# Reordering VectorE's queue in both mixers of a fused attention and MLP block, and deferring one late ScalarE evacuation

## The chip, the cores and the metric

The kernel runs on one core of a Trainium2 chip. The metric is the device time of one execution in microseconds (us), the median of several runs. One execution was also profiled; the profile's span runs from the first to the last instruction and is about 1.8 us shorter than the metric. All runs told of here were with a granted TensorE clock of 0.999 to 1.0.

## The reference

The block is a linear attention layer followed by a token-mixing MLP, each behind a layer norm and with a residual. The change touches only the MLP:

```python
h = _layernorm(x)                                    # x: (1, 2048, 1024)
u = gelu(jnp.einsum("bsd,sf->bdf", h, w1) + b1)      # "mixer 1", 2048 -> 3584
y = jnp.einsum("bdf,fs->bds", u, w2) + b2            # "mixer 2", 3584 -> 2048
out = residual + y.transpose(0, 2, 1)
```

## The kernel before

Both mixers use a seven-product scheme in place of eight: each output block of 256x1024 is made from seven matrix products, some of which take sums or differences of operand blocks. VectorE makes those operand sums. Two output blocks form a "quad". Products 1, 5 and 3 of a quad are split once more into seven inner products of half width, for both blocks together; these are in1, in5 and in3 (mixer 1 also has in2). "Product 3 of in5" is the third-numbered inner product of outer product 5. Quads are numbered from 0, as in the code; quad 0 of mixer 2 uses no inner products, so quads 1, 2 and 3 are the three that the text speaks of there. Between the inner products, steps of an ordinary product of 512 columns fill TensorE.

The names in the profile: `sa` is an operand sum of an outer product (`asum(6)` in the code makes the one of product 6), `is` of an inner one, `wq` and `w2o` are weights, `gs` and `gi` (mixer 2) and `hi` (mixer 1) are sums on the moving side, `psI` holds the inner products in PSUM, `psA`, `psB`, `psC` the outer ones, `e`, `t` and `t1a` are partial sums in SBUF, `ot` is an output tile. Where its sum lies in `psA` or `psC`, it is made by an evacuation on ScalarE (a copy out of PSUM with the bias added) and then an addition of the residual `hr` on VectorE.

The inner products, in the order in which they are issued (cut):

```python
class Inner:
    def i1(self):   # ... a and b are the two halves that products 1, 2 and 6, 3 accumulate in
        ae = psz.tile([P, BANK], F32, tag="z0", ...); bc = psz.tile([P, BANK], F32, tag="z1", ...)
        # mixer 2 (banks == 2): a and e share one PSUM bank, b and c share another
        self.a, self.e, self.b, self.c = ae[:, 0:HW], e[:, HW:CW], bc[:, 0:HW], bc[:, HW:CW]
        self.mm(1, self.a, True)
        act.copy(self.b, self.a)
    # ... i6, i2, i5 ...
    def i7(self):
        self.mm(7, self.c, False)
        self.sink_sum(1, 1, self.c, self.es[:])      # VectorE addition that reads c
    def i3(self):
        self.mm(3, self.b, False)                    # TensorE writes b, in c's bank
        self.sink_sum(0, 1, self.b, self.es[:])
```

The interleaving. At each named point, deferred work ("late") is flushed if the point is listed, and then the action for that point is issued; numbers are stretches of filling steps:

```python
for f in (n.i1, "b", 0, n.i6, "c", n.i2, "2", 1, n.i5, n.i7, "7", 2, n.i3, "third", 3, n.i4, "end"):
```

One quad of mixer 2 (cut). VectorE's instructions keep the order in which they are written here:

```python
def run2(self, pend, on_p4, on_p7, cut, third_sums):
    def starting():
        self.asums(5)                  # sa, for both blocks
        self.in5 = self.inner(5)
        self.in5.sums()                # four is
        self.asums(6)                  # sa, for both blocks
        # ...
    self.interleave(self.in1, self.steps(*[st.p4 for st in pend]),
                    {"b": starting}, (("b", None), ("7", None), ("end", None)))
    on_p4()                            # two gs differences and their corrections
    # ...
    self.asums(7)                      # two wq differences, in place
    self.interleave(self.in5, self.steps(*[st.p6 for st in sts]))
    # ... asums(3), in3's sums, product 7 ...
    halves[0]()                        # a gs difference
    self.interleave(in3, self.steps(*[st.p2 for st in sts]),
                    {"2": halves[1], "7": begin_next, "third": before_last, ...}, (("7", None),))
```

The whole kernel:

## Time and profile before

| | before |
|---|---|
| time, median of the 3 runs not profiled | 567.18 us (566.92 to 568.14) |
| profiled span | 566.1 us |
| TensorE busy | 556.7 us, 98% |
| VectorE busy | 448.5 us, 79% |
| ScalarE busy | 287.6 us, 51% |
| gaps in TensorE's stream from 232 us on (why from there: last section) | 5.26 us |

The first part of the page gives engine, busy us, share of the span and instructions:

```profile
span 566.1 us, 8738 instructions
PE 556.7 (98%) x3278; PEld 309.8 (55%) x3278; DVE 448.5 (79%) x853; ACT 287.6 (51%) x609; POOL 1.8 (0%) x8
```

A TensorE that is busy 98% of the time looks as if 9 us were left, but pipelined matmuls overlap in the records (one of 512 columns is recorded as 379 ns long, and the next starts 216 ns after it), so the share says little about what is left. The Trainium skill says the same ("Perfetto Trace Analysis", section "Identifying the Most-Contended Engine": matmul busy share is not a good measure of how near TensorE is to its limit), and proposes other measures. Its section "Optimization Strategy" says to find the gaps between slices on the engine and what blocks it there. That is what we do. In the timeline, a group of n matmuls that starts at s should be followed by the next at s + n x pitch. The pitch is 0.216 us for 512 columns and 0.109 us for 256 (14 matmuls of 512 columns take 3.02 us, 14 of 256 take 1.53 us in the chain of waits). Whatever the next start lies beyond that is a gap.

The timeline of TensorE in mixer 2 (start, duration, engine, line, operation, output and inputs, count; in brackets the idle time before and what ended it):

```profile
439.97 1.24 PE L229 MATMUL psC<-gs,wq 128*128 128x512 f16 x5
442.11 0.92 PE L229 MATMUL psI<-gE,is 128*128 128x256 f16 x7 [0.90 <-DVE psA L229]
...
466.82 1.67 PE L229 MATMUL psA<-gO,w2o 128*128 128x512 f16 x7
469.42 0.92 PE L229 MATMUL psI<-gO,is 128*128 128x256 f16 x7 [0.93 <-DVE e L229]
...
470.94 1.24 PE L229 MATMUL psA<-gO,w2o 128*128 128x512 f16 x5
472.51 0.93 PE L229 MATMUL psI<-gO,is 128*128 128x256 f16 x7 [0.32 <-DVE e L229]
...
482.82 1.24 PE L229 MATMUL psC<-gs,w2o 128*128 128x512 f16 x5
484.17 0.92 PE L229 MATMUL psI<-gE,is 128*128 128x256 f16 x7
...
494.48 1.24 PE L229 MATMUL psB<-gT,sa 128*128 128x512 f16 x5
495.56 0.93 PE L229 MATMUL psI<-gE,is 128*128 128x256 f16 x7
```

The first pair reads: 439.97 + 5 x 0.216 = 441.05, the next group starts at 442.11, so the gap is 1.06 us. In the same way the others are 1.09, 0.49 and 0.27 us (and once more 0.27 us in quad 3, at 524.66). The last pair has no gap: 494.48 + 1.08 = 495.56. The gap of 0.27 us at 484.17 has no bracket, because the modelled ends of the matmuls before it cover it: counts and pitches find it, idle time does not.

In quad 1 of mixer 1 the same reading gives 0.52 us at 257.52 and 0.78 us at 279.21, and another 0.19 us at 275.16:

```profile
255.92 1.24 PE L229 MATMUL psC<-hT,wq 128*128 128x512 f16 x5
257.52 0.60 PE L229 MATMUL psI<-hi,is 128*128 128x256 f16 x4 [0.35 <-ACT psI L229]
...
278.00 0.59 PE L229 MATMUL psC<-hT,sa 128*128 128x512 f16 x2
279.21 0.60 PE L229 MATMUL psI<-hi,sa 128*128 128x256 f16 x4 [0.61 <-DVE t L229]
```

These gaps add up to 4.67 us: 0.52 + 0.19 + 0.78 in mixer 1, and 1.06 + 1.09 + 0.49 + 0.27 + 0.27 in mixer 2. The rest of the 5.26 us are seven gaps of 0.08 to 0.09 us.

At 257.52 TensorE waits for a copy of `psI` on ScalarE that stands behind a gelu, which itself waited for VectorE:

```profile
256.47 0.72 ACT L229 ACTIVATE gE<-e,b_sb 128x512 f16<-128x512 f32 x1 [0.61 <-DVE e L229]
257.10 0.36 ACT L229 COPY psI<-psI 128x256 f32<-128x256 f32 x1
```

The timeline of VectorE shows what stands in front of the additions that TensorE waits for, and where VectorE itself stands idle:

```profile
439.63 2.08 DVE L229 TENSOR_TENSOR sa<-sa,wq 128x1792 f16<-128x1792 f16 x2
441.64 0.42 DVE L229 TENSOR_TENSOR psA<-psI,es 128x256 f32<-128x256 f32 x1
...
445.31 0.42 DVE L229 TENSOR_TENSOR ot<-ot,hr 128x512 bf16<-128x512 bf16 x1 [1.80 <-ACT ot L480]
445.65 2.02 DVE L229 TENSOR_TENSOR gs<-gT,gE 128x3584 f16<-128x3584 f16 x1
...
467.02 2.01 DVE L229 TENSOR_TENSOR gs<-gO,gT 128x3584 f16<-128x3584 f16 x1
468.95 0.41 DVE L229 TENSOR_TENSOR e<-psI,e 128x256 f32<-128x256 f32 x1
...
476.96 0.42 DVE L229 TENSOR_TENSOR ot<-ot,hr 128x512 bf16<-128x512 bf16 x1 [0.45 <-ACT ot L480]
...
494.90 0.41 DVE L229 TENSOR_TENSOR e<-psI,es 128x256 f32<-128x256 f32 x1
```

The addition at 441.64 ends at 442.06, and product 3 starts at 442.11. It stood behind two `sa` sums that nobody needed yet. Product 3 writes the other half of the bank that this addition reads, and TensorE stands idle for 0.90 us before it. The Trainium skill ("PSUM — Partial Sum Buffer", section "PSUM bank collisions raise a hardware error") says to guard PSUM by bank (strictly, by bank and quadrant of partitions) and not by address; the wait in this trace fits that. In in3 the `e` addition at 468.95 ends at 469.36, behind a `gs` difference of 2 us, and the matmuls at 469.42 wait for it.

### The profile page before, as it was taken

To read this page: it belongs to the slowest core of one execution; us is meant where nothing else is said; L and a number is where in the kernel's file an instruction comes from. 1 tells how busy PE (TensorE), PEld (TensorE's weight loads), DVE (VectorE), ACT (ScalarE), POOL (GpSimd) and SP (SyncE) were. 2 spreads that over 40 slices of the span, in tenths; PEclk is the share of its full clock that TensorE was granted. 3 is DMA by queue.
4 is the path that set the end of the run, shared out by engine and by line. 5 is a ranking of instruction groups with operands and counts; after the bars stand their busy time and mean duration, and the time that the engine had idled before them with its cause. 6 is when DMAs were issued, how large, how long until landed. Compare 5 with 4: busy or idle time off the path is not lost.

```text
span 566.1 us, 8738 instructions
## 1 busy us (share of the span) xinstructions
PE 556.7 (98%) x3278; PEld 309.8 (55%) x3278; DVE 448.5 (79%) x853; ACT 287.6 (51%) x609; POOL 1.8 (0%) x8
## 2 busy tenths in 40 slices
PE   8999999999999999999999999999999999999997
PEld 3444444454444444456666766666445655656654
DVE  6898888544776788888989789888997889879783
ACT  4747777766766877635546465555211312313212
POOL 1000000000000000000000000000000000000000
PEclk9999999999999999999999999999999999999999
DMA  9833342115764862104041340431946644643111
GB/s 303 292 75 75 77 91 38 19 53 191 213 213 122 252 187 77 72 1 129 23 148 30 120 150 1 149 81 51 251 127 180 168 115 127 168 132 111 37 38 56
DMA packets 86217, 67.15 MB, mean 119 GB/s; under 512 B 15890, under 2 KB 80160, under 8 KB 86176
## 3 DMA queue, kind: packets, MB, share of 16 engines
q1 hardware_dynamic: 85440, 65.94, 39.9%
q10 hardware_dynamic: 672, 0.66, 0.3%
q8 instruction: 25, 0.41, 0.3%
q14 instruction: 16, 0.13, 0.1%
q0 software_dynamic: 64, 0.01, 0.0%
HBM read 54.54 MB, written 8.91 MB: 112 GB/s over the span
## 4 chain that ended last, share of the span: by engine, by line
PE 84%; DVE 10%; DMA 3%; issue 1%; ACT 1%; SPq 0%; DVEq 0%; ACTq 0%
PE psI L229 19%; PE acc_t L229 18%; PE psC L229 11%; PE psB L229 8%; PE psB L904 4%; PE psC L904 4%; PE psA L904 4%; PE psA L229 4%; DVE sa L229 2%; PE acc_t L1179 2%; PE psE L904 2%; DVE is L229 2%; PE psC L341 2%; PE psA L341 2%; PE acc_t L828 2%; DMA wkv<-in_A_wqkv_dram 1%
## 5 line engine op out<-in xcount | busy, mean ns | idle before, releaser
L229 PEld LDWEIGHTS <-is 128*128 128x128 f16 x652 | 63.6, 98 | 33.2 <-issue 5.6
L229 PEld LDWEIGHTS <-sa 128*128 128x128 f16 x606 | 59.3, 98 | 28.8 <-issue 0.9
L229 PEld LDWEIGHTS <-wq 128*128 128x128 bf16 (+1 forms) x503 | 49.2, 98 | 32.6
L229 PE MATMUL acc_t<-wo_sb,pqT 128*128 128x512 f16 x256 | 55.6, 379 | 0.0
L229 PE MATMUL acc_t<-xnT,wq_sb 128*128 128x512 bf16 x192 | 43.4, 379 | 0.0
L229 PEld LDWEIGHTS <-pqT 128*128 128x128 bf16 x256 | 25.0, 98 | 30.5 <-issue 0.6
L191 DVE TENSOR_SCALAR e_sb<-e_sb 128x512 bf16<-128x512 bf16 x64 | 18.5, 290 | 28.8 <-ACT e_sb L187 28.2
L187 ACT ACTIVATE e_sb<-acc_t 128x512 bf16<-128x512 f32 x40 | 23.9, 597 | 24.6 <-PE acc_t L229 12.0
L904 PEld LDWEIGHTS <-xs 128*128 128x128 f16 x208 | 20.0, 98 | 23.4 <-DVE xs L890 1.3
L229 PE MATMUL psC<-gs,wq 128*128 128x512 f16 x140 | 32.0, 379 | 0.0
L229 PE MATMUL psC<-hT,sa 128*128 128x512 f16 x112 | 31.2, 379 | 0.0
L229 PEld LDWEIGHTS <-wq_sb 128*128 128x128 bf16 x192 | 18.5, 98 | 23.0 <-issue 1.3
L229 PE MATMUL psI<-hi,is 128*128 128x256 f16 x200 | 30.0, 272 | 0.4 <-ACT psI L229 0.4
L229 PE MATMUL psB<-hT,sa 128*128 128x512 f16 x112 | 29.7, 379 | 0.0
L229 DVE BATCH_NORM_STATS2 hst<-acc_t 128x6 f32<-128x512 f32 x32 | 21.4, 692 | 9.1 <-ACT h_bf L229 8.9
L904 PE MATMUL psA<-wkv,xnT 128*128 128x512 bf16 x104 | 26.7, 379 | 0.0
L904 PEld LDWEIGHTS <-xnT 128*128 128x128 bf16 x156 | 15.3, 98 | 18.5 <-issue 0.2
L229 PE MATMUL psC<-hT,wq 128*128 128x512 f16 x96 | 24.6, 379 | 0.0
L229 ACT CAST h_bf<-acc_t 128x512 bf16<-128x512 f32 x32 | 18.4, 582 | 11.9 <-PE acc_t L229 11.2
L229 ACT COPY psI<-psI 128x256 f32<-128x256 f32 x50 | 17.9, 359 | 11.7 <-PE psI L229 10.6
L188 ACT ACTIVATE r_sb<-acc_t 128x512 bf16<-128x512 f32 x40 | 23.7, 593 | 0.0
L828 PE MATMUL acc_t<-wkv,xnT 128*128 128x512 bf16 x96 | 21.6, 379 | 0.9 <-ACT xnT L1081 0.9
(224 smaller groups left out, 1075.1 us busy)
## 6 DMA issues: line engine op xcount, KB each, us to landing
wq<-in_B_w_dram SPq DMA_DIRECT2D x14, 1024.0 KB, 7.8
wq<-in_B_w_dram SPq DMA_DIRECT2D x12, 896.0 KB, 6.4
xr<-in_A_x_dram SPq DMA_DIRECT2D x16, 256.0 KB, 5.8
rdb<-rd_dram SPq DMA_DIRECT2D x32, 128.0 KB, 3.9
h_dram<-h_bf SPq DMA_DIRECT2D x16, 256.0 KB, 2.0
hr<-h_dram SPq DMA_DIRECT2D x32, 128.0 KB, 3.2
out_dram<-ot SPq DMA_DIRECT2D x31, 128.0 KB, 2.1
x_sb<-in_A_x_dram SPq DMA_DIRECT2D x15, 256.0 KB, 3.1
```

Of the source, the lines that this page charges most:

```text
L187: pin(nc.scalar.activation(e_sb[:], src, ACT.Exp))
L188: pin(nc.scalar.activation(r_sb[:], src, ACT.Relu))
L191: pin(nc.vector.tensor_scalar(e_sb[:], e_sb[:], 1.0, PHI_EPS, ALU.min, ALU.add))
L229: return (lambda *a, **kw: pin(op(*a, **kw))) if self.always or getattr(Held, self.key) else op
L341: pe.matmul(ps[:, cols], lhsT=lhs[:, k, :], rhs=mv(k)[:, cols], start=(start and k == 0), stop=(k == self.nk - 1), skip_group_check=True,)
L828: mm = nc.tensor.matmul(pp[:, 0:CW], lhsT=xnT[:, kt, i * P:(i + 1) * P], rhs=wkv[:, kt, c * CW:(c + 1) * CW], start=(kt == 0), stop=(kt == ...
L904: pin(nc.tensor.matmul(ps[:], lhsT=lhs[:, k, :], rhs=rhs[:, k, :], start=(start and k == 0), stop=(k == hk2 - 1), skip_group_check=True,))
L1179: nc.tensor.matmul(qp[:, 0:SW], lhsT=wq_sb[:, kt, j * P:(j + 1) * P], rhs=xnT[:, kt, u * SW:(u + 1) * SW], start=(kt == 0), stop=(kt == ND ...
```

## The change

The intent is to keep operand sums that are needed late out of the way of additions that TensorE waits for. Sums of four are issued in halves, some of them behind those additions; the `gs` differences of in3 move one point later; of the two `sa` of `asum(6)` the second moves to the end of in1; and the gelu of mixer 1's first quad, second block, goes behind the next copy of `psI`. At point "b" of in1 only one deferred action is now flushed (`self.early`, 1, and 0 in quad 1, where none is waiting), so in quads 2 and 3 one `ot` addition, the one at 476.96 above, also goes behind the `psA` addition. No arithmetic is added. TensorE's order is unchanged; ScalarE's changes in that one place. The diff (cut to its core):

```diff
@@ run2
             def starting():
+                self.in1.sums(slice(2, 4))
                 self.asums(5)
                 self.in5 = self.inner(5)
-                self.in5.sums()
-                self.asums(6)
+                self.in5.sums(slice(0, 2))
+                sts[0].asum(6)
                 ...
             self.interleave(
-                self.in1, self.steps(*[st.p4 for st in pend]), {"b": starting}, (("b", None), ("7", None), ("end", None))
+                self.in1, self.steps(*[st.p4 for st in pend]),
+                {"b": starting, "7": lambda: self.in5.sums(slice(2, 4))}, (("b", self.early), ("7", None), ("end", None)),
             )
+            sts[1].asum(6)
             on_p4()
             ...
-            def before_last():
-                if nxt is not None:
-                    nxt.in1.sums(slice(2, 4))
-                sts[0].evac(0, 1, sts[0].e)
-
             def begin_next():
                 if nxt is not None:
                     nxt.in1 = nxt.inner(1)
                     nxt.in1.sums(slice(0, 2))
-
-            halves[0]()
+                sts[0].evac(0, 1, sts[0].e)
+
             self.interleave(in3, self.steps(*[st.p2 for st in sts]), {
-                "2": halves[1], "7": begin_next, "third": before_last,
+                "2": halves[0], "7": halves[1], "third": begin_next,
@@ run_first (mixer 1, first quad)
-            for st in sts:
-                st.p3()
+            sts[0].p3()
+            sts[1].p3_mm()
+            self.late.append(sts[1].p3_evac)
@@ run1 (mixer 1, second quad only: third_sums are the four sums on hO, "hi")
-                third_sums(slice(0, 2))
+                third_sums(slice(0, 3))
             ...
-            if third_sums is not None:
-                third_sums(slice(2, 3))
             ...
-                "b": nop if third_sums is None else lambda: third_sums(slice(3, 4)),
+                "7": nop if third_sums is None else lambda: third_sums(slice(3, 4)),
```

More of the change, by code (lines that the diff above doesn't have):

```diff
@@ L503, in __init__ @@
             self.S = {}
+            self.early = 1
         def cols(self, h):
@@ L1619 @@
     nxt = next2(1)
+    nxt.early = 0
     run_all(make_t4)
@@ L1622 @@
     nxt.in1 = nxt.inner(1)
-    nxt.in1.sums()
+    nxt.in1.sums(slice(0, 2))
     for st in pend:
```

## The prediction

> What bounds it. TensorE: the page's first part gives it 556.7 of 566.1 us (98%), VectorE 79%. Busy share can't say what is left, so I read the PE timeline. Matmuls start 0.109 us apart (256 columns) or 0.216 us (512); a gap is what a group's start lies beyond the start before plus count times pitch. Where the change acts I find:
> - mixer 1, quad 1: 0.52 us at 257.5 (copy of psI queued on ScalarE behind the late gelu), 0.19 at 275.2, 0.78 at 279.2 (VectorE "t" additions behind two "hi" sums);
> - mixer 2, quad 1: 1.06 at 442.1 (inner product 3 of in1, waits for the psA addition), 1.09 at 469.4 and 0.49 at 472.5 (in3, "e" additions behind a 2 us "gs" difference);
> - mixer 2, quads 2 and 3: 0.27 each at 484.2 and 524.7 (psA addition behind "sa" and "is").
> Together 4.67 us: the change cannot win more. The waits are for whole banks: product 3 writes one half of a PSUM bank whose other half the addition reads. That fits the Trainium skill, "PSUM — Partial Sum Buffer", section on bank collisions (guard by bank, not address); the trace shows 0.90 us of such idle at 442.1.
>
> What the change does. No arithmetic is added, PE's order stays; VectorE's instructions are permuted. Start to start in the VectorE timeline: is pair 1.1-1.2 us, sa 1.0, gs 1.95, inner addition 0.34, hi 0.6-0.7.
>
> Ledger:
> 1. Late gelu deferred: psI copy goes at about 256.1; 0.52 closes.
> 2. sums3: two hi leave the way of the t additions; 0.19 closes. But the fourth hi now stands after product 7's addition and product 4 needs it, about 0.5 us too late; of 0.78 only 0.25 is won. Items 1 and 2: about 0.95.
> 3. in1 of mixer 2: one sa and one is pair leave from before the psA addition: 1.06, 0.27, 0.27 close.
> 4. in3: gs goes behind the additions: 1.09 and 0.49 close; product 4 now needs the third addition, done just in time (margin under 0.05).
> 5. New cost. The second sa of asum(6) now comes after the ot addition that waits for ScalarE's last product-4 evacuation (idle 1.80 before it, each quad). That idle is not filled; instead gs, its corrections, two wq differences and the psI+es addition of in5 start 1.0 us later against PE. Before, from PE's last product-4 matmul to that addition's end takes 8.9 us, and product 3 of in5 follows after 9.1 (486.4 to 495.6): slack 0.2. So a gap of about 0.8 opens there in each of 3 quads: -2.45.
>
> Sum: 0.95 + 1.60 + 1.58 - 2.45 = about 1.7 us won: quad 1 gains about 1.8, quads 2 and 3 lose about 0.55 each.
>
> Predicted time: 565.5 us, range 563.3 to 567.0 (8 in 10). Faster by over 2%: 0.5%; within 2%: 99%; slower: 0.5%.
>
> What would show it. The gaps at 257.5, 442.1, 469.4, 472.5, 484.2, 524.7 gone from the PE timeline; about 0.5 us left near 278 with hi as cause; new waits of about 0.8 us on VectorE "e" at product 3 of in5 in all three quads of mixer 2; the mixer-2 quad period growing from 40.5 to about 41. VectorE busy unchanged.
>
> What would make it wrong. If the in5 addition has more slack than I read (ScalarE's evacuation earlier, so that idle is filled), the win is up to 4 us (563). If product 4 in in3 misses its margin, or output transfers hold a buffer, 0.3 to 1 us is lost per quad and the time is unchanged or slightly worse (567). The spread of runs before (566.92 to 568.14) is nearly the effect.

## The result

| | before | after |
|---|---|---|
| time, median of 4 runs each | 567.53 us (566.92 to 568.14) | 565.93 us (565.45 to 566.11) |
| profiled span | 566.1 us | 564.1 us |
| TensorE gaps from 232 us on | 5.26 us | 3.56 us |
| VectorE busy | 448.5 us | 448.3 us |

The ratio is 0.997 with a 95% interval of 0.9953 to 0.9988: 1.6 us faster, which is clear of noise. A ratio in this document is the mean time of one kernel's fast runs over that of the other's in the same rounds, so it is not quite the ratio of the medians. The gaps fell by 1.70 us. Of the 2.0 us that the profiled span shrank, the other 0.3 us lie before the first changed instruction: a gap of 0.08 us that both kernels have stands at 243.57 us before and at 243.27 us after. That much the unchanged first part moves from run to run.

The time alone is less sharp than its median looks: the interval of the ratio allows a gain of 0.7 to 2.7 us. The kernel before was run 27 more times beside the experiments below, with a median of 567.2 us, 1.3 us above the changed kernel's 565.9, and its profiled run (567.89) was one of its slow ones. The gaps are the better evidence.

The first part of the page, after:

```profile
PE 555.1 (98%) x3262; PEld 310.0 (55%) x3278; DVE 448.3 (79%) x853; ACT 287.4 (51%) x609; POOL 1.8 (0%) x8
```

The busy shares are those of before. TensorE's timeline of mixer 2 at the five places shown above:

```profile
438.73 1.24 PE L229 MATMUL psC<-gs,wq 128*128 128x512 f16 x5
439.81 0.93 PE L229 MATMUL psI<-gE,is 128*128 128x256 f16 x7
...
465.32 1.67 PE L229 MATMUL psA<-gO,w2o 128*128 128x512 f16 x7
466.84 0.93 PE L229 MATMUL psI<-gO,is 128*128 128x256 f16 x7
...
468.37 1.24 PE L229 MATMUL psA<-gO,w2o 128*128 128x512 f16 x5
469.44 0.93 PE L229 MATMUL psI<-gO,is 128*128 128x256 f16 x7
...
479.76 1.24 PE L229 MATMUL psC<-gs,w2o 128*128 128x512 f16 x5
480.84 0.93 PE L229 MATMUL psI<-gE,is 128*128 128x256 f16 x7
...
491.15 1.24 PE L229 MATMUL psB<-gT,sa 128*128 128x512 f16 x5
493.04 0.92 PE L229 MATMUL psI<-gE,is 128*128 128x256 f16 x7 [0.65 <-DVE e L229]
```

The four gaps of before are gone: 438.73 + 1.08 = 439.81, and so on. In their place there is a new gap where there was none: 491.15 + 1.08 = 492.23, and product 3 of in5 starts at 493.04, 0.81 us late. It stands in each of the three quads (452.01, 493.04 and 534.07), 2.43 us together. The time from one to the next, which is the length of a quad, is 41.03 us; before, it was 524.66 - 484.17 = 40.49 us.

VectorE's timeline in that quad shows why:

```profile
480.03 0.43 DVE L229 TENSOR_TENSOR psA<-psI,es 128x256 f32<-128x256 f32 x1 [0.78 <-PE psI L229]
...
484.03 0.42 DVE L229 TENSOR_TENSOR ot<-ot,hr 128x512 bf16<-128x512 bf16 x1 [1.50 <-ACT ot L480]
484.38 1.08 DVE L229 TENSOR_TENSOR sa<-sa,wq 128x1792 f16<-128x1792 f16 x1
485.38 2.02 DVE L229 TENSOR_TENSOR gs<-gT,gE 128x3584 f16<-128x3584 f16 x1
...
492.57 0.42 DVE L229 TENSOR_TENSOR e<-psI,es 128x256 f32<-128x256 f32 x1
```

The addition at 480.03 now waits for TensorE and not for operand sums. But `ot` waits 1.50 us for ScalarE's evacuation, and `sa`, which needs nothing from ScalarE, stands behind it. So `gs` starts 1.0 us later than directly behind `ot`, and with it the whole run up to the addition at 492.57. That addition ends at 492.99, and product 3 starts at 493.04.

In mixer 1 the gap at 257.5 is gone (255.62 + 1.08 = 256.70). The gap of 0.78 us has become one of 0.56 us, with another releaser:

```profile
255.62 1.24 PE L229 MATMUL psC<-hT,wq 128*128 128x512 f16 x5
256.70 0.60 PE L229 MATMUL psI<-hi,is 128*128 128x256 f16 x4
...
276.98 0.59 PE L229 MATMUL psC<-hT,sa 128*128 128x512 f16 x2
277.97 0.60 PE L229 MATMUL psI<-hi,sa 128*128 128x256 f16 x4 [0.39 <-DVE hi L229]
```

### The profile page after: what moved, and what is told of

The parts are those of the page before. It is cut to its first block, busy times and chain, and to the rows that moved or that the text cites. A ratio compares the mean times of both kernels' runs of the same rounds, so it can differ in the third digit from the quotient of the medians.

```text
span 564.1 us, 8722 instructions
## 1 busy us (share of the span) xinstructions
PE 555.1 (98%) x3262; PEld 310.0 (55%) x3278; DVE 448.3 (79%) x853; ACT 287.4 (51%) x609; POOL 1.8 (0%) x8
## 4 chain that ended last, share of the span: by engine, by line
PE 91%; DVE 6%; ACT 1%; issue 1%; DVEq 0%
PE psI L229 20%; PE acc_t L229 18%; PE psC L229 15%; PE psB L229 6%; PE psA L229 4%; PE psC L902 4%; PE psB L902 4%; PE psA L902 4%; DVE gs L229 3%; PE acc_t L826 3%; PE psB L341 2%; PE psA L341 2%; PE acc_t L1177 2%; PE psE L902 2%; PE psC L341 2%; PE kvps L855 1%
```

## The experiments

The theory: the new in5 gap comes from the second `sa` of `asum(6)` standing behind an `ot` addition that waits. Rival A: it comes from the other moved pair, the second half of in5's `is` sums, or from ScalarE's evacuation or transfers as such. Rival B: the split of `asum(6)` is what cured in1, so the gap is its price. All kernels below gave correct results. "Before" ran beside them, with medians of 567.1 to 567.2 us.

**e1: undo the split of asum(6).** Diff against the changed kernel:

```diff
-                sts[0].asum(6)
+                self.asums(6)
...
-            sts[1].asum(6)
             on_p4()
```

> Undo one part of the change: both sa operand sums of asum(6) again ahead of the psA addition; all else as after. My theory (the second sa behind an ot addition that waits for ScalarE makes the new gap): the 0.81 us gap at product 3 of in5 vanishes in all three quads, and because the is pair is now out of the way the psA addition still ends in time (computed 480.64 against 480.84 in the trace after), so no gap comes back at product 3 of in1, or under 0.05 us. Sum: 2.4 us under after, about 563.5 us. Rival A (the other part of the reordering, the second is pair of in5 moved behind the psA addition, or ScalarE/DMA, makes that gap): the in5 gaps stay at 0.8 and the time stays near 565.9. Rival B (the split of asum(6) is what cured in1): the 0.27 gaps at in1 come back, 0.5 to 1.5 us lost again.

Measured: 563.39 us (5 runs), ratio to before 0.9932 (0.992 to 0.9945). No in5 gap is left, and none came back at in1. Rivals A and B fall: with the rest of the change in place the split was not needed to cure in1, and it made the new gap.

**e2: swap two instructions.** The second `sa` is issued at the point "third", so that it stands directly ahead of the waiting `ot` and not behind it. Nothing else in any engine's order differs from the changed kernel.

```diff
-                {"b": starting, "7": lambda: self.in5.sums(slice(2, 4))}, (("b", self.early), ...
+                {"b": starting, "7": lambda: self.in5.sums(slice(2, 4)), "third": lambda: sts[1].asum(6)},
+                (("b", self.early), ...
             )
-            sts[1].asum(6)
```

> The only change in any engine's order against after: the second sa of asum(6) stands ahead of the ot addition that waits for ScalarE instead of behind it (six rows swap in the VectorE order). My theory: sa fills 1.0 of the 1.5 us idle there, gs starts 1.0 us earlier against PE, the three 0.81 us gaps at product 3 of in5 vanish: 2.4 us under after, about 563.5 us; VectorE busy unchanged. Rival A (is pair, or ScalarE or transfers): gaps stay, about 565.9 us.

Measured: 563.86 us (5 runs), ratio 0.9941 (0.9928 to 0.9953). VectorE busy is 448.3 us, as after. The VectorE timeline of the same quad:

```profile
482.02 1.08 DVE L229 TENSOR_TENSOR sa<-sa,wq 128x1792 f16<-128x1792 f16 x1
483.61 0.43 DVE L229 TENSOR_TENSOR ot<-ot,hr 128x512 bf16<-128x512 bf16 x1 [0.51 <-ACT ot L480]
483.95 2.02 DVE L229 TENSOR_TENSOR gs<-gT,gE 128x3584 f16<-128x3584 f16 x1
...
491.15 0.42 DVE L229 TENSOR_TENSOR e<-psI,es 128x256 f32<-128x256 f32 x1
```

And TensorE's:

```profile
490.73 1.24 PE L229 MATMUL psB<-gT,sa 128*128 128x512 f16 x5
491.81 0.93 PE L229 MATMUL psI<-gE,is 128*128 128x256 f16 x7
```

The idle time before `ot` shrank from 1.50 to 0.51 us, because `sa` ran in it. The addition ends at 491.57, before product 3 is due at 490.73 + 1.08 = 491.81. All three gaps are gone, for the same work. e1 and e2 differ by 0.5 us in the median; 0.23 us of that stands in their profiles at 243.4 us already, ahead of anything that differs, and from there on both have the same gaps, so we read no difference between them.

**e3: undo the other half.** The second `is` pair of in5 goes back ahead of the `psA` addition; the second `sa` stays late.

```diff
-                self.in5.sums(slice(0, 2))
+                self.in5.sums()
...
-                {"b": starting, "7": lambda: self.in5.sums(slice(2, 4))}, (("b", self.early), ...
+                {"b": starting}, (("b", self.early), ...
```

> Undo the other half of the in1 reordering: the second is pair of in5 again ahead of the psA addition, the second sa left late. My theory: the psA addition ends about 480.67 against 480.84 needed, so no gap at product 3 of in1; the in5 gaps of 0.8 stay in all three quads because gs still waits for ot and then sa: same time as after, 565.9 within 0.3 us. Rival A (this half makes the in5 gap): gaps vanish, about 563.5 us.

Measured: 566.16 us (4 runs), ratio 0.998 (0.9965 to 0.9996). Three gaps of 0.82 us at in5, none at in1. So, with the rest of the change in place, moving either the `is` pair (e1) or the one `sa` (e3) away from the `psA` addition was enough in these profiles; the change did both, and only the second had a price. Two limits apply. The margins are small: counting the 0.05 us that pass from the end of such an addition to the start of the matmul, it ends 0.15 to 0.20 us before it is needed in e1 and 0.09 to 0.13 us in e3, against 0.33 us in the changed kernel, where VectorE besides waits over 0.7 us for TensorE. And in quads 2 and 3 the `ot` addition stayed moved in every run that was built on the changed kernel. It alone took its wait of 0.45 us and its 0.34 us (start to start) from in front of the `psA` addition, more than the gap of 0.27 us, so by this estimate it may have sufficed there; no run tests it.

**e4: double the suspected cost.** The late `sa` is computed twice in place.

```diff
             sts[1].asum(6)
+            dve.tensor_tensor(sts[1].lhs[6], sts[1].lhs[5], sts[1].a11, ALU.subtract)
             on_p4()
```

> Double the suspected cost: the late second sa is computed twice in the same place (same values, correct result). My theory: gs and the in5 addition start another 1.0 us later against PE, and each of the three gaps grows from 0.81 to about 1.8 us: 3.0 us over after, about 568.9 us. If the gap has another cause, the extra VectorE work goes into idle time and the time stays within 0.5 us of after.

Measured: 569.21 us (4 runs), ratio 1.0036 (1.0022 to 1.005), 3.3 us over the changed kernel's 565.93.

```profile
450.06 1.24 PE L229 MATMUL psB<-gT,sa 128*128 128x512 f16 x5
453.08 0.92 PE L229 MATMUL psI<-gE,is 128*128 128x256 f16 x7 [1.78 <-DVE e L229]
```

Each gap is now 1.94 us (450.06 + 1.08 = 451.14, to 453.08), 1.13 us more than with one `sa`. The two `sa` take 2.21 us there from the first's start to the second's end, against 1.08 us for one. So VectorE's time at this place passes into TensorE's stream one for one.

**e10: leave sa, move the waiting instruction.** The `ot` addition that waits is deferred into in5; `sa` stays late.

```diff
-                ... (("b", self.early), ("7", None), ("end", None)),
+                ... (("b", self.early), ("7", None)),
```

> The second sa stays late, just ahead of gs as in the changed kernel; instead the ot addition that waits for ScalarE's last product-4 evacuation moves away from in front of it, to behind product 7's addition of in5. My theory (not the sa itself, but its place behind a waiting instruction of an in-order queue costs the time): VectorE goes on with sa and gs during the former 1.5 us of idle, all three in5 gaps vanish, 2.4 us under after, about 563.5 us. Rival (the late place of sa, or the length of sa plus gs, is the cause): the gaps stay at 0.8 us, 565.9.

Measured: 563.44 us (4 runs), ratio 0.9932 (0.9917 to 0.9947). No in5 gap. VectorE's timeline:

```profile
481.81 1.08 DVE L229 TENSOR_TENSOR sa<-sa,wq 128x1792 f16<-128x1792 f16 x1
482.81 2.02 DVE L229 TENSOR_TENSOR gs<-gT,gE 128x3584 f16<-128x3584 f16 x1
...
490.79 0.42 DVE L229 TENSOR_TENSOR e<-psI,es 128x256 f32<-128x256 f32 x1 [0.70 <-PE psI L229]
```

Now the addition waits for TensorE again. It was not the late place of `sa` as such, nor the length of `sa` plus `gs`; it was `sa` behind an instruction that waits, in a queue that is worked off in order. The Trainium skill states that VectorE's queue is one in-order queue ("DVE: scalar operands, raw-bit mode, write accounting and state across instructions", section "Flops that outlive an instruction"); the 1.50 us of idle with a ready `sa` behind it agree.

**e5: the deferred gelu alone, on the kernel before.**

```diff
-            for st in sts:
-                st.p3()
+            sts[0].p3()
+            sts[1].p3_mm()
+            self.late.append(sts[1].p3_evac)
```

> One part alone on the kernel before: only the late evacuation of mixer 1's first quad is deferred. My theory: the 0.52 us gap at 257.5 closes and nothing gives it back, because VectorE waits for TensorE twice (0.71 and 0.61 us) between there and the t additions; the other gaps of before stay (0.19, 0.78, 1.06, 1.09, 0.49, 0.27, 0.27). Time 0.5 us under before, about 566.7. Rival: the saved time is lost at once, the gap at 275 or 279 grows by as much, and the sum of the gaps is unchanged.

Measured: 566.67 us (4 runs) against 567.12, ratio 0.9994 (0.9979 to 1.0008). By the time alone this is inconclusive, since half a microsecond is as large as the scatter of the runs. The trace decides: the gap at 257.5 is gone, those of 0.19 and 0.78 us are as before. The rival falls. One thing was not expected: the gap at product 3 of in1 in quad 1 of mixer 2, 1.06 us before, is 0.63 us here, though nothing near it was changed. The VectorE work in front of it starts with an `is` sum that waits for a weight load. Measured from the start of the product-3 matmuls before it (the group of 28 on psB), that `is` starts 430.73 - 426.65 = 4.08 us later in the profile of before and 428.79 - 425.15 = 3.64 us later here, 0.44 us sooner, which is the difference of the gaps. So part of that one gap is the luck of a transfer's landing. In the other ten profiles this delay is 3.5 to 4.0 us, so the profile of before is at the late end.

**e6: undo the order of gs alone, in the changed kernel.**

```diff
+            halves[0]()
             self.interleave(in3, self.steps(*[st.p2 for st in sts]), {
-                "2": halves[0], "7": halves[1], "third": begin_next,
+                "2": halves[1], "third": begin_next,
```

> Undo the gs order alone in the changed kernel: the two gs differences again ahead of the e additions in in3. My theory: in quad 1 the gaps of 1.09 and 0.49 us at in3 come back, none in quads 2 and 3 (there VectorE reached the e addition before TensorE in the kernel before); the in5 gaps of 0.8 stay; 1.6 us over after, about 567.5 us. If gs behind the additions costs something elsewhere (product 4 of in3), less than 1.6 comes back.

Measured: 567.15 us (4 runs), ratio 1.0003 (0.9989 to 1.0016): all of the change's gain is gone. In the trace the gaps of 1.09 and 0.49 us are back in quad 1 and in no other quad; the in5 gaps stay at 0.81 us. The term is as computed, 1.58 us in the gaps; the time is 1.2 us over the changed kernel's, from other rounds.

**e7: the fourth hi earlier.** In the changed kernel the gap at 277.97 names `hi` as its releaser. Here that sum is issued after product 2, and an addition on `psC` makes room.

```diff
-                "7": nop if third_sums is None else lambda: third_sums(slice(3, 4)),
+                "2": nop if third_sums is None else lambda: third_sums(slice(3, 4)),
...
-            }, (("b", 1), ("c", None)))
+            }, (("b", 1), ("c" if third_sums is None else "7", None)))
```

> On the changed kernel: the fourth hi sum of mixer 1's first run1 is issued after product 2 instead of after product 7, and the e addition of psC moves behind product 7's addition to make room. My theory (the 0.56 us gap at 278 is product 4 waiting for the fourth hi): the gap falls to under 0.1 us, 0.5 us under after, about 565.4. Rival (it waits for the t addition of product 7): the gap stays or grows.

Measured: 565.69 us (4 runs), ratio 0.9973 (0.9959 to 0.9987). The gap of 0.56 us is gone, so it was the wait for `hi`. But half of it came back 2 us later: product 6 of the next in1 starts 0.28 us late, because the copy of `psI` on ScalarE now stands behind a gelu whose input was delayed by the swap (it starts at 279.77). The net 0.28 us cannot be told from noise in the time.

**e8: e2 and e7 together.**

> The second sa ahead of the waiting ot addition (as in the run that swapped those two) and the fourth hi early (as in the run beside this one): gaps at 278 and at product 3 of in5 all gone, sum 0.56 + 2.43 = 3.0 us under after, about 562.9 us, and about 4.5 us (0.8%) under before.

Measured: 563.00 us (5 runs, 562.66 to 563.18), ratio 0.9925 (0.9911 to 0.9938). Gaps from 232 us on: 0.88 us. As expected but for the 0.28 us of e7.

**e9: as e8, and one gelu behind that copy.**

```diff
-                "third": gelu(0, 1, self.t3), "end": gelu_late(1, 1, self.t3),
+                "third": (gelu if third_sums is None else gelu_late)(0, 1, self.t3), "end": gelu_late(1, 1, self.t3),
```

> The run with both repairs, and in addition the gelu of the sum of product 3 in that one stretch moves behind ScalarE's next psI copy. My theory: the 0.28 us gap that the earlier fourth hi left at product 6 of the next quad's in1 came from that copy standing third behind two gelus (start 279.77, TensorE ready at about 279.0); with one gelu behind it, it starts about 279.2 and the gap closes. About 0.3 us under the run with both repairs, 562.7 us, no gap over 0.1 us from 232 us on. Rival: the gelus only move, and a later copy (of psI after product 6, or of t1a) makes a gap of the same size.

Measured: 562.86 us (5 runs), ratio 0.9923 (0.991 to 0.9935). The gap of 0.28 us is gone and a new one of 0.13 us stands at 284.58, 4.4 us further on, at the first filling matmul on `psB`. It starts 0.04 us after the end of a ScalarE copy of `t1a` into `psB` (284.16 + 0.38 = 284.54), the kind of copy that the rival named; that this copy holds it up is read from the trace and the code, and no run tests it. So the theory and the rival were each half right, and the time does not tell e9 from e8. Gaps from 232 us on: 0.72 us. Both versions beat both kernels, by 4.1 to 4.4 us against before (medians of the same rounds) and by about 3 us against the changed kernel.

## Why the prediction was right

It forecast 1.7 us; 1.6 us were measured in the time and 1.70 us in the gaps. That the time agrees to 0.1 us is partly luck, as its interval is 2 us wide, and forecast and gaps start from the same profile of before, in which one weight load landed late. The gaps opened and closed where it said. Point by point:

1. *Late gelu, 0.52 us.* Right; the gap is gone, and e5 shows it for this part alone in the trace.
2. *Sums of hi.* Right: 0.19 closed, and of 0.78 us 0.22 were won (0.25 forecast), the rest turned into a wait for the fourth `hi`. e7 shows that cause.
3. *in1, 1.06 + 0.27 + 0.27 us.* The gaps closed. But three details were not in the prediction: either of the two moves that it names would have done in these profiles (e1, e3); in quads 2 and 3 an `ot` addition moved too, and its share was not separated; and of the 1.06 us some 0.44 us depended on when a weight load landed (e5). The credit given to the change in quad 1 is good for this pair of profiles only.
4. *in3, 1.58 us.* Right, to 0.01 us, by e6. The narrow margin at product 4 held; no gap appeared there.
5. *The new cost, 2.45 us.* Right: 3 x 0.81 = 2.43 us. e2 shows that the place behind the waiting `ot` causes it, e10 that moving `ot` cures it as well, e4 that the dose counts, e1 that the split could be left out altogether.

So the question for this change is where the expected gain went. Of 4.67 us that the change could win, 4.11 were won (all but the 0.56 us at 277.97), and 2.43 were given back at one new place. Without that place the same change gives 3.4 to 3.8 us (e1, e2: medians against before in the same rounds).

The rule behind point 5 was arithmetic on the trace alone. In the profile of before, TensorE was through with in1's last product-4 matmuls at 486.44. From there VectorE needed 8.87 us to the end of the in5 addition (494.90 + 0.41 = 495.31), and TensorE came to the matmul that waits for it after 9.12 us (495.56). With the 0.05 us from such an addition's end to the matmul's start, the slack was 0.2 us. Adding 1.0 us to such a chain costs 0.8 us.

## What to carry to other kernels

When an instruction is moved out of the way in an in-order queue, look at what it lands behind and at what stands behind it there: work that is ready must not stand behind an instruction that waits for another engine, since the idle time then goes unused and everything after it is late. Before moving, read from the trace the slack of the next place where the bottleneck engine waits for this queue, and compare it with the length of what is moved. On an engine that is busy 98% of the time, count matmuls times pitch between starts; the busy share was the same in a version with 5.3 us of gaps and in one with 3.6.

## What the Trainium skill lacked or had wrong

- "TensorE: Matmul & The Clock Gate", section "Back-to-back issue gap", says that in a real kernel of weight load and matmul pairs the spacing at 512 columns is about 131 ns, and that the formula of an isolated matmul over-counts there. In this kernel, which is such a stream of pairs, the spacing is 216 ns at 512 columns (14 in 3.02 us) and 109 ns at 256 (14 in 1.53 us), which is that formula (columns / 2.4 + 2.5 ns).
- "VectorE: DVE Perf Modes", section "The DRAIN you can't avoid", gives no size for the difference between a following instruction that uses the result and one that does not. In these traces an `is` sum of 0.62 us is followed after 0.54 us by an independent one and after 0.66 us by one that reads its result.
- We found no page that says that single matmul records can be missing, though their weight loads are recorded, and then look like gaps: the profile of after has 3262 matmuls where that of before has 3278, for the same program order and 3278 weight loads in both, and before 232 us it shows several gaps of 0.21 to 0.22 us, just one matmul of 512 columns, that the other does not show. Gaps were therefore compared only from 232 us on.
